# A Fourier mixing layer and a gated feed-forward: DFT-47 of five batches moved into the token steps, and bank claims of two columns

## The chip, the cores and the metric

One core of a Trainium2 chip runs the whole program. The metric is device time in microseconds (us), the median of three runs: 2581.76 us (2578.75 to 2582.05). TensorE (PE) does the matrix products and its weight loads (PEld); VectorE (DVE), ScalarE (ACT) and GpSimd (POOL) work on data between them; SyncE (SP) issues almost all DMAs.

## The reference

Two layers in a row, cut to what matters:

```python
X = np.fft.rfft(x, axis=1)                      # x: 8 batches, 3008 positions, 256 features
Yr = Xr @ w_r - Xi @ w_i + b_r
Yi = Xr @ w_i + Xi @ w_r + b_i
Yr = np.sign(Yr) * np.maximum(np.abs(Yr) - 0.01, 0.0)      # Yi likewise
y = np.fft.irfft(Yr + 1j * Yi, n=3008, axis=1)
h = y.reshape(24064, 256) @ w_in                # w_in: 256 x 2048
out = (h / (1 + np.exp(-1.702 * h))) @ w_out    # w_out: 2048 x 256
```

## The kernel before

The transform of 3008 positions is split into 64 x 47. For one batch it runs in five steps: a DFT of length 47 (step A, `dft47`, L463), whose result goes to a DRAM tensor s1; a DFT of length 64 (step B, products `pa<-kr,br`), which reads s1 back into tiles br; the mixing matrices with the threshold; the inverse DFT of length 64, whose result goes to a DRAM tensor s2; and the inverse DFT of length 47, which is part of `tokens` (L604). `tokens(u)` takes eighth u of all batches' tokens (NU = 8 a batch) from s2 into the transposed tiles th and tl of the feed-forward.

The feed-forward (`Ffn`) goes over 47 blocks of 512 tokens and, in each, over 8 groups of 256 hidden features. `up` makes 12 products of 512 columns into two banks of PSUM (`pa<-th,wi_h` and the like), ScalarE applies the activation, VectorE and ScalarE form sums and split each into a high and a low part (fp32r), and `down` makes 21 products of 256 columns into accumulators po. The last loop (L863) makes 376 such steps. The spectral steps of the next batch stand in a list with a cost each (`spectral`, L478), and the loop takes from it in proportion to the feed-forward steps left, so that the batch is done 16 steps before it is needed. For batches 3 to 7 that list begins with the eight groups of step A at a cost of 1100 each and an empty step of cost 4000. Step A of batches 1 and 2 runs in the start-up (`early`, `do_early`).

Products of small shape run on quarters of the array: `dft47` uses 48 rows by 64 columns in four quarters (four products of 512 columns, in two passes since they are fp32), `tokens` the same with 32 products of 47 columns. Inside `with quarters()` PE's order is the one written. All else is ordered when the program is built: a scheduler places the recorded instructions of each engine by its own timeline, so that products of several stages mix.

The pool `pa` has four banks of PSUM. `bank()` takes one; an instruction that first writes it waits until ScalarE and VectorE have read what was there. So that this wait isn't met inside a quarters group, `claim` (L351) makes a tiny product into the first bank ahead of the group: two columns of output on all 128 rows, with a weight load of 128 columns. `dft47` and `tokens` need two banks each and claim one of them.

Input tiles of step A (xt), of the tokens (ur), and the pairs of the inverse step share three buffers of the tag sx.

Of the kernel before, what the change touches and what calls it, by code (L numbers as in the profile page):

```python
# [25 lines left out]
NU = NJ // 4  # L26
# [90 lines left out]
def fourier_mix_then_gated_ffn(ctx: ExitStack, tc: tile.TileContext, x, w_r, w_i, b_r, b_i, w_in, w_out, pack, kbs, out):  # L117
# [232 lines left out]

    def claim(ps):  # L351

        mm(ps[:, 0:2], wi_h[:, 0, 0:128], wi_h[:, 0, 0:2])

    def dram_views(s1, s2):
        return (s1.rearrange("c (s r) p n j d -> c (r p n j) s d", r=2),
# [106 lines left out]
    def dft47(b, n, t, first=None, other=None):  # L463

        ps = [bank(), bank() if other is None else other]
        with quarters():
            if first:
                first(ps[0])
            for c, p in ((1, 1), (0, 0), (0, 1), (1, 0)):
                mm(ps[p][64 * c:64 * c + 64], kp[64 * p:64 * p + 48], t[c][64 * p:64 * p + 48])  # L470
        s1w = s1s[b].rearrange("c f p n j d -> (c f) p n (j d)")
        for p in range(2):
            ev = buf2("aev").rearrange("p j d -> p (j d)")
            nc.scalar.copy(ev, ps[p])  # L474
            nc.sync.dma_start(s1w[:, p, n], ev)


    def spectral(b, s2):  # L478
        begun = b in s1s
        if not begun:  # L480
            new_s1(b)
        s1r, s2w = dram_views(s1s[b], s2)
        ki, fg, wf_h, wf_l = (parts[n] for n in "ifhl")
        yd = dr.tile([NS, 2, N1, D], F32, name="yd")
        xs, raw, zs, ys = {}, {}, {}, {}

        def pair(name):
            t = buf([128, 2, 512], F32R, name, tag="sx", bufs=3)
            return t[:, 0], t[:, 1]

        def load_x(n):
            if n < 8 and n not in xs:
                xs[n] = xload(b, n, buf([128, 1024], F32, "xt", tag="sx", bufs=3))

        def stage_a(n):
            load_x(n)
            load_x(n + 1)
            dft47(b, n, xs[n], claim)

        def load_b(sp):  # L500

            k = buf([128, 2, 2 * N1], F32, "kr")
            t = buf2("br")
            nc.sync.dma_start(k, kbs[12 + sp])
            for c in range(2):
                nc.sync.dma_start(t[64 * c:64 * c + 64], s1r[c, :, 2 * sp:2 * sp + 2])
            raw[sp] = t, k

        def stage_b(sp):

            if sp == 0:
                load_b(0)
            if sp + 1 < 12:
                load_b(sp + 1)
            co = dft64(*raw.pop(sp))
            zz = buf([128, 2, 6, 128], F32R, "zz")
            split(zz[:, 0], zz[:, 1], co.rearrange("p c v n -> p (c v) n"))
            zs[sp] = zz

        def stage_mix(sp):  # L520

            zz = zs.pop(sp)
            pa, pb = bank(), bank()
            for v, ps in ((2, pa[:, 0:D]), (1, pb[:, 0:D]), (0, pb[:, D:])):
                for c in range(2):
                    mm3(ps, zz[:, 0, 3 * c + v], zz[:, 1, 3 * c + v], wf_h[:, v, c], wf_l[:, v, c], start=c == 0, stop=c == 1)
            v = mixed(pa, pb)
            threshold(v)
            for i in range(2):
                nc.sync.dma_start(yd[2 * sp + i].rearrange("r k e -> k r e"), v[64 * i:64 * i + 64])  # L530

        def load_y(sp):
            ys[sp] = buf2("yr")
            nc.sync.dma_start(ys[sp], yd[2 * sp:2 * sp + 2].rearrange("s r k e -> (r k) s e"))

        def split_y(sp):
            y = ys[sp]
            yh, yl = (t.rearrange("p (s d) -> p s d", s=2) for t in pair("yh"))
            for i in range(2):
                f = fg[:, 2 * sp + i:2 * sp + i + 1]  # L540
                nc.scalar.mul(yh[:, i], y[:, i], f)
                nc.vector.scalar_tensor_tensor(yl[:, i], y[:, i], f, yh[:, i].bitcast(F32), ALU.mult, ALU.subtract)
            ys[sp] = yh, yl

        def stage_inv(sp):
            yh, yl = ys.pop(sp)
            pv = bank().rearrange("p (s d) -> p s d", s=2)
            if sp == 0:
                for i in range(2):
                    mm3(pv[:, i], ki[:, 0, 1 - i], ki[:, 1, 1 - i], yh[:, i], yl[:, i])  # L550
            else:
                mm3(pv, ki[:, 0, 0], ki[:, 1, 0], yh, yl)
            ev = buf2("iev")
            nc.scalar.copy(ev, pv)
            nc.sync.dma_start(s2w[2 * sp:2 * sp + 2].rearrange("s p d -> p s d"), ev)

        steps = []

        def add(cost, step, n, count):
            if 0 <= n < count:  # L560
                steps.append((cost, lambda: step(n)))

        if not begun:
            add(0, load_x, 0, 8)
            for n in range(8):
                add(1100, stage_a, n, 8)
            steps.append((4000, lambda: None))
        for n in range(12 + 5):
            add(900, stage_b, n, 12)
            add(2000, stage_mix, n - 1, 12)  # L570
            add(0, load_y, n - 3, 12)
            add(0, split_y, n - 5, 12)
            add(650, stage_inv, n - 5, 12)
        return steps
# [16 lines left out]
    def first_tokens(u):  # L591
        t = us.pop(u)
        for c in range(2):
# [3 lines left out]
            for k in range(JP * u // TOK, (JP * (u + 1) - 1) // TOK + 1):  # L597
# [3 lines left out]
                n0, n1 = max(0, -a), min(JP, TOK - a)  # L601
                split(*(t2[:, c, a + n0:a + n1] for t2 in ytiles[k]), ps[:, n0:n1])

    def tokens(u):  # L604
        if u < 2:
            return first_tokens(u)
        t = us.pop(u)
        ps = [bank() for p in range(2)]
        pv = [b[:, :JP].rearrange("p (c j n) -> p c j n", c=2, j=4) for b in ps]
        with quarters():  # L610
            claim(ps[0])
            for j in range(4):
                for c in range(4):
                    i = 64 * (c % 2)
                    for p in reversed(range(2)):
                        hs = slice(64 * p, 64 * p + 48)
                        mm(pv[p][i:i + 64, c // 2, j], t[hs, j, 64 * c:64 * c + 64], kz[hs])
        for k in range(JP * u // TOK, (JP * (u + 1) - 1) // TOK + 1):
            if k not in ytiles:
                ytiles[k] = (fbuf([128, 2, TOK], F32R, "th"), fbuf([128, 2, TOK], F32R, "tl"))  # L620
            th, tl = ytiles[k]
            at = [JP * u + 94 * j - TOK * k for j in range(4)]
            js = [j for j in range(4) if 0 <= at[j] and at[j] + 94 <= TOK]
            for p in range(2):
                if js:
                    hi, lo = (t[:, :, at[js[0]]:at[js[0]] + 94 * len(js)].rearrange("p c (j n) -> p c j n", j=len(js))[:, :, :, 47 * p:47 * p + 47]
                              for t in (th, tl))
                    split(hi, lo, pv[p][:, :, js[0]:js[0] + len(js)])
                for j in range(4):
                    a = at[j] + 47 * p  # L630
                    n0, n1 = max(0, -a), min(47, TOK - a)
                    if j not in js and n0 < n1:
                        split(th[:, :, a + n0:a + n1], tl[:, :, a + n0:a + n1], pv[p][:, :, j, n0:n1])
# [133 lines left out]
    def tokens_to(n):  # L767
        nonlocal done
        while done < NB * NU and JP * done < n:
            load_u(done)  # L770
            load_u(done + 1)
            tokens(done)
            done += 1
        load_u(done)

    lx0, one0, a0, lk0, t0, b0, m0, i0 = first_batch(new_s2(0))
    new_s1(1)
# [85 lines left out]
    for n in range(NT * NQ):  # L863
        k, q = divmod(n, NQ)
        if q == 0:
            cur = Ffn(k)
        cur.up(q)
        if n < NQ:
            if n < 7:
                with after("h", "l"):  # L870
                    weights(9 + n)
            do_early(n)
            if n == 6:
                with after("h", "l"):
                    rounded_parts()
        elif not queue and nextb < NB:
            queue = spectral(nextb, new_s2(nextb))
            total, spent, n0 = sum(c for c, _ in queue), 0.0, n
            n1 = NQ * S * nextb // TOK - 16
            nextb += 1  # L880
        while queue and spent < total * (n + 1 - n0) / (n1 - n0):
            c, step = queue.pop(0)
            spent += c
            step()
        need = TOK * (1 + (n + 2) / NQ)
        while queue and need + JP > S * (nextb - 1):
            queue.pop(0)[1]()
        if JP * done < need:
            tokens_to(need)
        if behind is not None:  # L890
            behind[0].down(behind[1])
        behind = (cur, q)
# [36 lines left out]
```

## Time and profile before

| what | value |
|---|---|
| median of three runs | 2581.76 us |
| the profiled execution | 2581.11 us |
| its span, first to last instruction | 2579.3 us |
| granted TensorE clock | 0.996 |
| DMA queues of SyncE, share of the 16 engines | 28.1% |

The span is cut by the page into busy time of engines, the chain that ended last, groups of like instructions and DMA issues. A matmul's duration in it includes its way through the array; how long PE is taken by it is read from the distance between the starts of successive matmuls. The rows that matter are shown in the prediction.

### The profile page before, as it was taken

How to read it: one execution, taken by the hardware profiler on the slowest of the kernel's cores; microseconds unless marked ns; L12 is line 12 of the kernel's file. 1: busy time of each engine (PE TensorE's matmuls, PEld its weight loads, DVE VectorE, ACT ScalarE, POOL GpSimd, SP SyncE). 2: the span in 40 equal slices, each digit the busy share in tenths (PEclk: the TensorE clock that was granted, in tenths of full speed). 3: DMA queues.
4: the chain of work that ended last, by engine and by line, in shares of the span. 5: the costliest groups of instructions: out<-in, count | busy, mean ns of one | idle time of the engine just before them, and what ended most of it. 6: DMA issues, size and time to landing. Idle time of an engine off the chain costs nothing.

```text
span 2579.3 us, 49276 instructions
## 1 busy us (share of the span) xinstructions
PE 2556.0 (99%) x19885; PEld 2267.6 (88%) x19885; DVE 1915.7 (74%) x3240; ACT 1597.1 (62%) x2587; POOL 53.2 (2%) x63
## 2 busy tenths in 40 slices
PE   9899999999999999999999999999999999999999
PEld 7679989999899998999889998899988999889888
DVE  6588877777578775777767776678766787777776
ACT  4566665666666666666666666666666666655555
POOL 0000000000000000000000000000000000000000
PEclk9899999999999999999999999999999999999999
DMA  7653331222513235122341323322243122200000
GB/s 220 198 170 86 100 99 54 71 66 66 164 38 86 83 86 148 54 71 82 110 122 52 91 79 115 103 64 83 73 128 97 56 83 80 60 27 24 15 17 17
DMA packets 163780, 221.81 MB, mean 86 GB/s; under 512 B 18256, under 2 KB 121136, under 8 KB 163552
## 3 DMA queue, kind: packets, MB, share of 16 engines
q1 hardware_dynamic: 161920, 212.83, 28.1%
q0 software_dynamic: 1632, 5.83, 0.7%
q8 instruction: 156, 2.56, 0.4%
q14 instruction: 72, 0.59, 0.1%
HBM read 117.40 MB, written 101.19 MB: 85 GB/s over the span
## 4 chain that ended last, share of the span: by engine, by line
PE 96%; DVE 1%; ACT 1%; DMA 1%; issue 0%; SPq 0%; POOL 0%; POOLq 0%; DVEq 0%; ACTq 0%
PE pa L155 58%; PE po L155 37%; DMA s<-iev 0%; PE pi L155 0%; DMA wf_h<-s 0%; PE wm L155 0%; ACT gb L658 0%; DVE lt L663 0%; PE pt L395 0%; DMA pk<-in_pack 0%; ACT aev L474 0%; DVE lb L150 0%; DVE mv L414 0%; ACT iev L441 0%; DVE aem L283 0%
## 5 line engine op out<-in xcount | busy, mean ns | idle before, releaser
L658 ACT ACTIVATE gb<-pa 128x512 f32<-128x512 f32 x752 | 448.8, 599 | 433.0 <-PE pa L155 430.0
L150 DVE TENSOR_TENSOR lt<-gt,ht 128x1024 fp32r<-128x1024 f32 x367 | 452.1, 1232 | 262.1 <-ACT ht L149 261.0
L155 PE MATMUL pa<-th,wi_h 128*128 128x512 f32 x1504 | 594.1, 395 | 0.2
L155 PE MATMUL pa<-tl,wi_h 128*128 128x512 f32 x1504 | 591.4, 393 | 0.0
L155 PE MATMUL pa<-th,wi_l 128*128 128x512 f32 x1504 | 587.6, 391 | 0.0
L149 ACT CAST ht<-gt 128x1024 fp32r<-128x1024 f32 x367 | 384.4, 1047 | 182.9 <-DVE gt L691 179.7
L689 DVE TENSOR_TENSOR gt<-gb 128x512 f32<-128x512 f32 x367 | 253.2, 690 | 199.4 <-ACT gb L658 191.5
L150 DVE TENSOR_TENSOR lb<-gb,hb 128x768 fp32r<-128x768 f32 x367 | 353.5, 963 | 15.2 <-ACT hb L149 14.7
L155 PEld LDWEIGHTS pa<-th,wi_l 128*128 128x128 f32 x1504 | 283.2, 188 | 57.7
L155 PEld LDWEIGHTS pa<-th,wi_h 128*128 128x128 f32 x1504 | 284.1, 189 | 54.7 <-ACT gb L658 3.2
L149 ACT CAST hb<-gb 128x768 fp32r<-128x768 f32 x367 | 306.4, 835 | 31.3 <-PE po L155 22.2
L155 PEld LDWEIGHTS pa<-tl,wi_h 128*128 128x128 f32 x1504 | 284.4, 189 | 40.5
L155 PE MATMUL po<-lt,wo_0a 128*128 128x256 f32 (+1 forms) x752 | 206.1, 287 | 0.0
L155 PE MATMUL po<-ht,wo_1a 128*128 128x256 f32 (+1 forms) x752 | 204.8, 285 | 0.0
L155 PE MATMUL po<-lt,wo_0b 128*128 128x256 f32 (+1 forms) x752 | 204.0, 287 | 0.0
L155 PE MATMUL po<-ht,wo_1b 128*128 128x256 f32 (+1 forms) x752 | 203.1, 285 | 0.0
L155 PE MATMUL pa<-wf_h,zz 128*128 128x256 f32 x1008 | 202.9, 282 | 0.0
L155 PE MATMUL po<-ht,wo_0a 128*128 128x256 f32 (+1 forms) x752 | 182.3, 288 | 0.0
L155 PE MATMUL po<-ht,wo_0b 128*128 128x256 f32 (+1 forms) x752 | 173.0, 287 | 0.3 <-ACT ht L149 0.3
L155 PEld LDWEIGHTS pa<-wf_h,zz 128*128 128x128 f32 x1008 | 164.9, 189 | 1.4
L690 DVE TENSOR_TENSOR gt<-gb,gt 128x256 f32<-128x256 f32 x367 | 154.6, 421 | 6.9
L155 PE MATMUL po<-hb,wo_0a 128*128 128x256 f32 x552 | 157.6, 293 | 0.0
(170 smaller groups left out, 4663.2 us busy)
## 6 DMA issues: line engine op xcount, KB each, us to landing
s<-aev SPq DMA_DIRECT2D x112, 256.0 KB, 3.5
s<-iev SPq DMA_DIRECT2D x96, 256.0 KB, 2.5
ur<-s SPq DMA_DIRECT2D x124, 192.0 KB, 3.4
out<-o SPq DMA_DIRECT2D x93, 256.0 KB, 2.1
br<-s SPq DMA_DIRECT2D x168, 128.0 KB, 2.9
yd<-mv SPq DMA_DIRECT2D x168, 128.0 KB, 2.4
yr<-yd SPq DMA_DIRECT2D x84, 256.0 KB, 2.9
xt<-in_x SPq DMA_DIRECT2D x80, 192.0 KB, 3.4
```

The source lines that it names most:

```text
L149: nc.scalar.copy(hi, src)
L150: return nc.vector.tensor_tensor(lo, src, hi.bitcast(F32), ALU.subtract)
L155: last[0] = nc.tensor.matmul(ps, lhsT=w, rhs=t, start=start, stop=stop).ins
L658: done_at["g"] = nc.scalar.activation(o, ps.rearrange("p (h n) -> p h n", h=2), AF.Gelu_apprx_sigmoid).ins
L689: nc.vector.tensor_tensor(gt[:, 0:2], b12, gb[:, 0:3:2], ALU.subtract)
L690: nc.vector.tensor_tensor(gt[:, 2], gb[:, 2], gt[:, 0], ALU.subtract)
```

## The change

Three edits. First, `dft47` is taken apart into its products and its output, and `tokens` makes the products of step A for batch b + 2, eighth n, together with the inverse DFT of eighth n of batch b, in one quarters group; a new `load_x` loads their input one token step ahead. Second, `spectral` loses step A and the empty step behind it, and its list for batch 3 and later is made once the tokens of the batch two earlier are done. Third, a claim writes two rows of output instead of 128 (a weight load of two columns), and a merged group claims all four of its banks.

```diff
-        mm(ps[:, 0:2], wi_h[:, 0, 0:128], wi_h[:, 0, 0:2])
+        mm(ps[0:2, 0:2], wi_h[:, 0, 0:2], wi_h[:, 0, 0:2])
...
-            for c, p in ((1, 1), (0, 0), (0, 1), (1, 0)):
-                mm(ps[p][64 * c:64 * c + 64], kp[64 * p:64 * p + 48], t[c][64 * p:64 * p + 48])
+            dft47_products(ps, t)
+        dft47_out(b, n, ps)
+
+    def dft47_products(ps, t):
+        for c, p in ((1, 1), (0, 0), (0, 1), (1, 0)):
+            mm(ps[p][64 * c:64 * c + 64], kp[64 * p:64 * p + 48], t[c][64 * p:64 * p + 48])
+
+    def dft47_out(b, n, ps):
...
-        if not begun:
-            add(0, load_x, 0, 8)
-            for n in range(8):
-                add(1100, stage_a, n, 8)
-            steps.append((4000, lambda: None))
...
+    def load_x(u):
+
+        b, n = u // NU + 2, u % NU
+        if u >= NU and b < NB and u not in steps47:
+            if n == 0:
+                new_s1(b)
+            steps47[u] = b, n, xload(b, n, buf([128, 1024], F32, "xt", tag="sx", bufs=3))
...
+        step = steps47.pop(u, None)
+        if step:
+            b, n, _ = step
+            p47 = [bank() for p in range(2)]
         ps = [bank() for p in range(2)]
...
-            claim(ps[0])
+            for x47 in p47 + ps if step else ps[:1]:
+                claim(x47)
+            if step:
+                dft47_products(p47, step[2])
...
+        if step:
+            dft47_out(b, n, p47)
...
             load_u(done)
-            load_u(done + 1)
+            load_x(done)
+            if done < 2:
+                load_u(done + 1)
             tokens(done)
             done += 1
         load_u(done)
+        load_x(done)
...
-        elif not queue and nextb < NB:
+        elif not queue and nextb < NB and (nextb < 3 or done >= NU * (nextb - 1)):
```

PE, one group of step A of batch 3 before, on its own (`pa<-xt,kp`), and behind it a claim of 128 by 2 between whole products (`po<-..` are down products):

```order
L155 MATMUL pa<-xt,kp 64x512 x4
L155 MATMUL po_7107<-lt,wo_0b 128x256
L155 MATMUL po_7107<-ht,wo_1b 128x256
L155 MATMUL po_7108<-lt,wo_0b 128x256
L155 MATMUL po_7108<-ht,wo_1b 128x256
L155 MATMUL po_7107<-ht,wo_0b 128x256
L155 MATMUL po_7107<-lt,wo_0b 128x256
L155 MATMUL po_7107<-ht,wo_1b 128x256
L155 MATMUL pa<-wi_h 128x2
L155 MATMUL po_7109<-lt,wo_0b 128x256
L155 MATMUL po_7109<-ht,wo_1b 128x256
```

PE, a merged group after (step A of batch 5 with tokens of batch 3; `pa<-kz,ur` are the token products), with the claims ahead of it:

```order
L155 MATMUL pa<-wi_h 2x2 x2
L155 MATMUL po_12287<-hb,wo_0a 128x256
L155 MATMUL po_12287<-lb,wo_0a 128x256
L155 MATMUL po_12287<-hb,wo_1a 128x256
L155 MATMUL po_12287<-hb,wo_0a 128x256
L155 MATMUL po_12287<-lb,wo_0a 128x256
L155 MATMUL po_12287<-hb,wo_1a 128x256
L155 MATMUL pa<-wi_h 2x2
L155 MATMUL po_12287<-hb,wo_0a 128x256
L155 MATMUL pa<-wi_h 2x2
L155 MATMUL pa<-xt,kp 64x512 x4
L155 MATMUL pa<-kz,ur 64x47 x32
```

The products of step A now stand straight ahead of the token products, and four claims stand ahead of the group, at three places. In the built program a claim is an instruction on 128 rows by 32 columns of the array, where it was on 128 by 128; step A and the tokens are on 64 by 64.

SP, the end of step A and the first reads of step B, batch 3 before and batch 4 after (`s1<-aev` writes step A's result, `br<-s1` reads it back for step B):

```order
L475 DMA s1_7427<-aev_7937 128x512
L475 DMA s1_7427<-aev_7940 128x512
L506 DMA br_8201<-s1_7427 64x2x256 x2
L506 DMA br_8206<-s1_7427 64x2x256 x2
L589 DMA ur_8827<-s2_3853 48x1024 x2
```

```order
L455 DMA xt_11385<-in_x 48x1024 x2
L481 DMA s1_7666<-aev_11363 128x512
L481 DMA s1_7666<-aev_11366 128x512
L577 DMA ur_11885<-s2_7720 48x1024 x2
L499 DMA br_11441<-s1_7666 64x2x256 x2
L499 DMA br_11446<-s1_7666 64x2x256 x2
L499 DMA br_11462<-s1_7666 64x2x256 x2
```

The reads follow the last write as before. What moved is PE's side: after, between the last merged group of batch 4 and the first product of step B stand 12 up products and 21 down products, of which the last are these:

```order
L155 MATMUL po_11012<-ht,wo_1b 128x256
L155 MATMUL po_11011<-ht,wo_0b 128x256
L155 MATMUL po_11011<-lt,wo_0b 128x256
L155 MATMUL po_11011<-ht,wo_1b 128x256
L155 MATMUL po_11013<-ht,wo_0b 128x256
L155 MATMUL po_11013<-lt,wo_0b 128x256
L155 MATMUL po_11013<-ht,wo_1b 128x256
L155 MATMUL pa<-kr,br 128x2x64 x8
L155 MATMUL pa<-th,wi_h 128x512
```

Before, several feed-forward steps stood there. Now it is less than two of them.

More of the change, by code (lines that the diff above doesn't have):

```diff
@@ L478, in spectral @@
     def spectral(b, s2):
-        begun = b in s1s
-        if not begun:
-            new_s1(b)
         s1r, s2w = dram_views(s1s[b], s2)
@@ L484, in spectral @@
         yd = dr.tile([NS, 2, N1, D], F32, name="yd")
-        xs, raw, zs, ys = {}, {}, {}, {}
+        raw, zs, ys = {}, {}, {}
         def pair(name):
@@ L489, in pair @@
             return t[:, 0], t[:, 1]
[L491 to L498, printed above, removed]
         def load_b(sp):
@@ L561, in add @@
                 steps.append((cost, lambda: step(n)))
-        if not begun:
-            add(0, load_x, 0, 8)
-            for n in range(8):
-                add(1100, stage_a, n, 8)
-            steps.append((4000, lambda: None))
         for n in range(12 + 5):
@@ L602, in first_tokens @@
                 split(*(t2[:, c, a + n0:a + n1] for t2 in ytiles[k]), ps[:, n0:n1])
+    steps47 = {}
+    def load_x(u):
[4 more added lines that the diff above has]
+            steps47[u] = b, n, xload(b, n, buf([128, 1024], F32, "xt", tag="sx", bufs=3))
     def tokens(u):
```

## The prediction

> **What bounds the kernel now.** I read the page first (busy time by engine, then the chain that ended last), then busy time by stretches, and then the timeline of TensorE around single groups.
>
> ```profile
> span 2579.3 us, 49276 instructions
> PE 2556.0 (99%) x19885; PEld 2267.6 (88%) x19885; DVE 1915.7 (74%) x3240; ACT 1597.1 (62%) x2587; POOL 53.2 (2%) x63
> PE 96%; DVE 1%; ACT 1%; DMA 1%; issue 0%; SPq 0%; POOL 0%; POOLq 0%; DVEq 0%; ACTq 0%
> ```
>
> ```profile
> 700.00:1200.00 500.00, 499.58 (x4010) 450.37 (x4009) 377.34 (x635) 312.62 (x507) 8.38 (x9) 1.00 0.29 83
> ```
>
> The first numbers of the last row are the stretch, its length and PE's busy time: in 500 us PE idles 0.4. VectorE (377 us of 500) and ScalarE (313) have room, and the granted clock is 1.00. So no wait can be removed from the main stretch; what counts is what PE's own instructions cost, switches between tile shapes among it, and any new wait on PE goes to the end undiminished. The profiled execution took 2581.1 us, 0.7 below the median of the runs; the sum goes from 2581.1.
>
> **Prices of a switch.** Start of a group of DFT-47 products in the timeline, PE alone (start, duration, operation, rows*columns of the array, count):
>
> ```profile
> 655.74 0.52 PE L155 MATMUL po<-ht,wo_0b 128*128 128x256 f32 x3
> 656.19 0.66 PE L155 MATMUL pa<-xt,kp 48*64 48x512 f32 x4
> ```
>
> and its end, from a later window:
>
> ```profile
> 656.67 0.61 PE L155 MATMUL pa<-xt,kp 48*64 48x512 f32 x4
> 657.21 0.39 PE L155 MATMUL po<-lt,wo_0b 128*128 128x256 f32 x1
> 657.43 0.28 PE L155 MATMUL po<-ht,wo_1b 128*128 128x256 f32 x1
> 657.55 0.29 PE L155 MATMUL po<-lt,wo_0b 128*128 128x256 f32 x1
> ```
>
> Whole products of 256 columns follow each other at 0.12 us (657.43 to 657.55). The third of the x3 starts at 655.98, the group 0.21 later: **entering costs 0.09**. From the group's second pass (656.67) to the next whole product are 0.54 us, and that one's successor comes after 0.22: the **return costs 0.10** more, since the weight load was not done ahead. What the leaving itself costs shows where DFT-47 products once run straight into token products, without a switch:
>
> ```profile
> 130.05 0.59 PE L155 MATMUL po<-xr,kp 48*64 48x512 f32 x1
> ...
> 130.48 1.10 PE L155 MATMUL pa<-kz,ur 48*64 48x47 f32 x64
> 131.51 0.50 PE L155 MATMUL po<-ht,wo_0a 128*128 128x512 f32 x1
> ```
>
> 0.43 instead of 0.54: **leaving costs 0.11**. I take 0.095 for each change of shape, whichever way, and 0.10 for each return to whole products.
>
> **The claims.** One before, between whole products, and one directly ahead of a group:
>
> ```profile
> 658.03 0.28 PE L155 MATMUL po<-ht,wo_1b 128*128 128x256 f32 x1
> 658.15 0.17 PE L155 MATMUL pa<-wi_h 128*128 128x2 f32 x1
> 658.18 0.36 PE L155 MATMUL po<-lt,wo_0b 128*128 128x256 f32 x1
> 658.38 0.28 PE L155 MATMUL po<-ht,wo_1b 128*128 128x256 f32 x1
> ...
> 695.85 0.39 PE L155 MATMUL pa<-tl,wi_h 128*128 128x512 f32 x1
> 696.08 0.39 PE L155 MATMUL pa<-th,wi_l 128*128 128x512 f32 x1
> 696.30 0.17 PE L155 MATMUL pa<-wi_h 128*128 128x2 f32 x1
> 696.40 0.66 PE L155 MATMUL pa<-xt,kp 48*64 48x512 f32 x4
> ```
>
> The first one costs 0.03 + 0.08 = 0.11 us. The second costs nothing: 0.10 passes to the group, which is the price of the switch anyway. The new claim has two columns, and the built program gives it a shape of its own, 128 rows by 32 columns. The trace before has no such instruction. It has a change in the columns alone, from 64x128 (the inverse of the first batch) to 64x64, beside one to whole products:
>
> ```profile
> 43.47 0.60 PE L155 MATMUL pi<-mv,kt 64*128 64x256 f32 x4
> 43.99 0.48 PE L155 MATMUL pa<-wf,co 128*128 128x256 f32 x1
> ...
> 87.95 0.60 PE L155 MATMUL pi<-mv,kt 64*128 64x256 f32 x4
> 88.47 0.66 PE L155 MATMUL pa<-xp,kp 48*64 48x512 f32 x4
> ```
>
> Both take 0.52 us: a change of columns alone costs as much as a full one. So a new claim between whole products is bounded by 0.03 (its own step at 658.15, no switch) from below and by two changes and a return, 2 x 0.095 + 0.10 = 0.29, from above; less than nothing is excluded, as an instruction stays. I take 0.29 and 0.01 for its short load, since the 64x128 rows are the nearest. The Trainium skill, "TensorEngine Tiling (Array Packing)", Key Properties, says that a change of the tiling mode, unlike one of the tile, drains TensorE. By it the new claim pays 0.29, as in the sum; without it the same 158 stretches of claims would be almost free, which is rival C.
>
> **Sum on PE.** Counted in the built programs: changes of shape 294 before, 451 after (49 fewer entries into quarters, as 40 groups merge and fewer token groups are cut; 156 more into claims from whole products). Returns to whole products 145 before, 193 after. Claims 114 before, 56 of them between whole products; 194 after, in 158 stretches. So: 157 x 0.095 = +14.9; 48 x 0.10 = +4.8; 56 x 0.11 = -6.2; own steps of the new claims 158 x 0.01 + 36 x 0.03 = +2.7. Together **+16.2**. In it the merging alone gives -49 x (2 x 0.095 + 0.10) = -14.2; the claims take it back. The DFT products themselves, their copies and DMAs are the same in number and only stand elsewhere.
>
> **The wait that appears.** Before, the spectral steps of batches 3 to 7 left a step of cost 4000 with no work between the last DFT-47 and the first use of its result. It goes. The chain (ScalarE's copies, the write to DRAM, the read back, the first product of step B) in the timeline of batch 3:
>
> ```profile
> 697.87 1.07 ACT L474 COPY aev<-pa 128x512 f32<-128x512 f32 x2
> ```
>
> ```profile
> 698.48 0.83 SPq L475 DMA_DIRECT2D s<-aev  x2
> 702.45 3.08 SPq L506 DMA_DIRECT2D br<-s  x4
> ```
>
> ```profile
> 719.84 0.27 PE L155 MATMUL pa<-kr,br 128*128 128x128 f32 x1
> ```
>
> ```profile
> DMA to landing us min/median/max: 2.5/2.9/5.3
> ```
>
> From the group's start (696.40) to the first read's issue 6.05 us (batch 7: 1954.21 to 1960.35, 6.14). A tile br needs two reads; the second of the four is issued 0.65 later, the fourth 1.95. With 2.9 to landing the first tile is there at 6.05 + 0.65 + 2.9 = 9.6 and the second at 10.9. Before, the product came at 23.4, so all was hidden.
>
> ```profile
> 1954.21 1.09 PE L155 MATMUL pa<-xt,kp 48*64 48x512 f32 x8
> ```
>
> ```profile
> 1960.35 1.25 SPq L506 DMA_DIRECT2D br<-s  x2
> ```
>
> After, PE's work from the group's start to that product is the DFT products (0.91, that is 0.48 + 0.43), 32 token products (1.03, row 130.48), the return 0.10, 12 up products at 0.23 (2.8; spacing at 695.85) and 16, 21, 23, 25 and 17 down products at 0.12 for batches 3 to 7: 6.8, 7.4, 7.6, 7.8 and 6.9 us. PE therefore waits 2.8, 2.2, 2.0, 1.8 and 2.7, together 11.5. The next tile's products stand right behind (at most four whole products between), wanted at 10.1 to 10.5 and there at 10.9: some 3 more. **+14.5**, with 12.5 at a landing of 2.5 and 26 at 5.3. SP's queue holds this too: ahead of the reads stand two loads xt, the two writes and two loads ur, which fit into the 6 us. Behind the waiting products stand all other PE work, so nothing refills the gap.
>
> **Four banks at once.** The merged group holds all four banks. 18 of the 40 groups are followed at once by an up product that needs the bank of the first copied half.
>
> ```profile
> 660.02 1.09 PE L155 MATMUL pa<-xt,kp 48*64 48x512 f32 x8
> ```
>
> ```profile
> 661.18 1.08 ACT L474 COPY aev<-pa 128x512 f32<-128x512 f32 x2 [1.37 <-PE pa L155]
> ```
>
> ```profile
> L149 ACT CAST ht<-gt 128x1024 fp32r<-128x1024 f32 x367 | 384.4, 1047 | 182.9 <-DVE gt L691 179.7 <-PE pa L155 0.5
> ```
>
> An undelayed copy ends 1.75 us after the group's start (661.18 + 0.59), and the token products run until 1.95: hidden. A cast on ScalarE ahead of it costs up to 1.05. From 0 to 18 x 1.05 = 19; I take a quarter of the cast each, **+4**, as ScalarE is busy 62% but mostly with shorter pieces. The claims' own waits for banks lie behind down products (21 x 0.12 = 2.5 us a step), as before: 0.
>
> **Moved at no cost.** The loads xt are issued a token step ahead (a median of 270 products of PE, before 60), and hold one of the three buffers that they share with ur and the pairs of the inverse step. One is left for 12 pairs in the 310 us of a batch, one in 26 us, so I put this at 0; without that cover 60 inverse products could wait up to a cast, 1.05 us, each, and that belongs to D.
>
> Sum: 16.2 + 14.5 + 4 = +34.7, so 2615.8; I say **2615**.
>
> **Rivals.** B, the switches cost as said but the read is hidden (it lands sooner than the copies suggest): 2581.1 + 16.2 + 4 = 2601. Against it: 6.05 us to the issue alone leave at most 1.8 for issue and landing, and the shortest landing is 2.5.
>
> C, the other side: the claim of 32 columns changes no shape that must drain. For it: the weight load is two columns wide, and the old claim's whole cost was its load. Then the quarters save 14.2, the old claims 6.2, and the new ones cost 194 x 0.01 to 0.03, 2 to 6. With the waits at 11 (14.5 less 5 x 0.3, the copies as early as at 661.18, and 5 x 0.4, landings at 2.5; no bank wait) the time is 2581.1 - 18.4 + 11 = 2574, faster; with all 18.5 of waits 2585. It decides from a claim below 0.05 us, where the 11 and the savings cancel. The section LDWEIGHTS of "TensorE: Matmul & The Clock Gate" in the Trainium skill puts a load at its columns over 1.2 ns, so estimated 1.7 ns for two against 107 for 128; by that alone C would hold, and no row before shows a load of two columns. Against C stand the two equal 0.52.
>
> D, the four banks bind: each of 40 groups makes PE wait half a microsecond more for ScalarE: +20, 2635. For it: 36 claims now stand in pairs or threes, which wait for several banks at one place. Against it: the 0.4 us of idle in 500.
>
> That the change doesn't do what it says: two of the 40 groups stand cut in the program after two token products; that is 2 x 0.29 and in the counts.
>
> **How the numbers follow.** A 0.62, B 0.13, C 0.12, D 0.13. A by itself spans 2603 to 2628 (landing and bank waits at their ends). The range leaves out C and the far part of D: 2594 to 2640. 0.2% is 5.2 us, about what a measurement of this kernel can tell from no change. C splits into faster 0.07 and same 0.05; slower takes A, B and D, 0.88, of which I leave 0.02 to same and 0.01 to faster for what I didn't see.
>
> **What would show it.** Right: whole product to 2x2 claim 0.21 and claim to whole product about 0.10, with 0.22 behind it; some 2 to 3 us of PE idle put down to DMA br before kr,br at five places, some 310 us apart; DFT to token products 0.42. Wrong: claims 0.03 apart from their neighbours (C); no idle before kr,br (B); idle at claims or at up products behind groups put down to ScalarE, over 10 us in sum (D).

## The result, and the profile after

The changed kernel took 2600.49 us (median of 6 runs, 2598.17 to 2601.95), the kernel before in the same runs 2580.64 (2578.75 to 2582.05). The ratio is 1.0074 with a 95% interval of 1.0063 to 1.0086: slower, by 20 us where 34 were forecast.

The page of the changed kernel, its head and its chain:

```profile
span 2596.4 us, 49412 instructions
PE 2551.6 (98%) x19965; PEld 2268.4 (87%) x19965; DVE 1923.4 (74%) x3240; ACT 1595.8 (61%) x2587; POOL 52.2 (2%) x63
...
PE 76%; DVE 2%; DMA 2%; ACT 1%; issue 1%; SPq 0%; POOL 0%; POOLq 0%; DVEq 0%; ACTq 0%
PE pa L155 46%; PE po L155 30%; DMA s<-aev 1%; DMA br<-s 1%; DVE lb L150 0%; DVE gt L696 0%; ACT ht L149 0%; ACT gb L665 0%; ACT aev L480 0%; DVE lt L150 0%; ACT yh L534 0%; DVE tl L150 0%; DVE gt L698 0%; DVE gt L697 0%; DMA xt<-in_x 0%
```

The span grew by 17.1 us while PE was busy 4.4 us less. The chain of before was 96% PE; now write and read of step A's result (`s<-aev`, `br<-s`) stand in it with 1% each. The stretch of the main part says the same, 494.06 us busy of 500 where it was 499.58 (columns as in the prediction):

```profile
700.00:1200.00 500.00, 494.06 (x3999) 443.06 (x3998) 371.05 (x620) 310.67 (x501) 8.89 (x9) 1.00 0.30 88
```

What PE waited for, from the list of waits (us in total, times, the longest):

```profile
PE pa L155 <- DMA br<-s: 14.0, 5, 3.5
...
PE po L155 <- DVE o L763: 3.0, 6, 1.1
...
PE po L155 <- ACT o L756: 2.4, 2, 1.2
...
PE po L155 <- DVE o L762: 1.6, 2, 1.1
...
PE po L155 <- DVE o L759: 0.8, 1, 0.8
PE pa L155 <- ACT aev L480: 0.7, 1, 0.7
```

and from the same list of the kernel before, the two lines that answer the first and the last:

```profile
PE pa L155 <- DMA br<-s: 0.7, 1, 0.7
PE pa L155 <- ACT aev L474: 0.7, 1, 0.7
```

Five waits for the read-back of step A are the largest item, and of a kind that was forecast. The lines `po <- o` were not: a down product there waits until the last block's accumulators are copied out. The line `aev`, where a wait for the four banks would show, has its one wait of before. Claims and a merged group, in the timeline of PE (the claim's tile of 128 x 32 is printed 128*2):

```profile
1063.65 0.28 PE L155 MATMUL po<-hb,wo_1a 128*128 128x256 f32 x1
1063.77 0.17 PE L155 MATMUL pa<-wi_h 128*2 128x2 f32 x1
1063.80 0.36 PE L155 MATMUL po<-hb,wo_0a 128*128 128x256 f32 x1
1064.23 0.17 PE L155 MATMUL pa<-wi_h 128*2 128x2 f32 x1
1064.33 1.09 PE L155 MATMUL pa<-xt,kp 48*64 48x512 f32 x8
1065.24 1.10 PE L155 MATMUL pa<-kz,ur 48*64 48x47 f32 x64
1067.43 0.39 PE L155 MATMUL po<-hb,wo_0a 128*128 128x256 f32 x1 [1.10 <-DVE o L763]
```

The claim comes 0.12 us after the whole product and passes to the next one in 0.03; nothing drains. And it costs what the 128-column claim cost: the product behind it still shows 0.36 us. Directly ahead of the group it is again free (0.10 to the group), though this one comes some 0.2 us late: 0.43 behind a product that the next usually follows after 0.20. The merged group ends in a wait of 1.10 us for VectorE, of the unforeseen kind.

An account of PE makes this whole. The distances between successive starts of matmuls, from 175 us on, were sorted by what stands there: entries, exits and small products of quarters; claims; what exceeds the usual distance by over 0.15 us (waits); the rest. The account is of the two profiled executions, 2598.17 and 2581.11 us, whose spans are 17.1 us apart; the medians are 19.9 apart.

| us | before | after | difference | forecast |
|---|---|---|---|---|
| quarters, with entry and return | 135.5 | 116.7 | -18.8 | -14.2 |
| claims | 6.6 | 12.6 | +6.0 | +30.4 |
| waits at `kr,br` | 1.1 | 15.0 | +13.9 | +14.5 |
| other waits | 2.6 | 15.3 | +12.7 | +4 |
| the rest, with the start | 2423.7 | 2427.1 | +3.4 | 0 |

The claims' forecast is the +16.2 of the switches less the merge's -14.2. The rest holds a surprise, told last: a lower clock behind some waits.

### The profile page after: what moved, and what is told of

Same layout as the page of the kernel before. It is cut to its first block, busy times and chain, and to the rows that moved or that the text cites. A ratio compares the mean times of both kernels' runs of the same rounds, so it can differ in the third digit from the quotient of the medians.

```text
span 2596.4 us, 49412 instructions
## 1 busy us (share of the span) xinstructions
PE 2551.6 (98%) x19965; PEld 2268.4 (87%) x19965; DVE 1923.4 (74%) x3240; ACT 1595.8 (61%) x2587; POOL 52.2 (2%) x63
## 4 chain that ended last, share of the span: by engine, by line
PE 76%; DVE 2%; DMA 2%; ACT 1%; issue 1%; SPq 0%; POOL 0%; POOLq 0%; DVEq 0%; ACTq 0%
PE pa L155 46%; PE po L155 30%; DMA s<-aev 1%; DMA br<-s 1%; DVE lb L150 0%; DVE gt L696 0%; ACT ht L149 0%; ACT gb L665 0%; ACT aev L480 0%; DVE lt L150 0%; ACT yh L534 0%; DVE tl L150 0%; DVE gt L698 0%; DVE gt L697 0%; DMA xt<-in_x 0%
```

## The experiments

Each was timed in five rounds against the kernel before; the figure is the median, then the ratio with its interval. Waits are sums from the same account.

**The short claim alone**, in the kernel before:

```diff
-        mm(ps[:, 0:2], wi_h[:, 0, 0:128], wi_h[:, 0, 0:2])
+        mm(ps[0:2, 0:2], wi_h[:, 0, 0:2], wi_h[:, 0, 0:2])
```

> The kernel before with the claims of two columns alone (nothing merged, no step moved). Theory 1 (from the trace after, where a claim between whole products takes 0.12 to its start, 0.03 to the next product and 0.20 behind it, as before): a claim costs 0.11 us in either form, so the time stays within 0.1% of before and a lone claim keeps the 0.03 and 0.20. Theory 2 (of the prediction, a drain at each change to 128 rows by 32 columns): about 56 x 0.18 + 57 x 0.1, some 15 us more, +0.6%. Theory 3 (the short load saves the claim): 56 x 0.08 = 4.5 us less.

2579.11 us, 0.9991 [0.9983, 1.0]. Its claims take 6.5 us in the account, the old ones 6.6. Timeline of PE:

```profile
656.11 0.28 PE L155 MATMUL po<-ht,wo_1b 128*128 128x256 f32 x1
656.23 0.17 PE L155 MATMUL pa<-wi_h 128*2 128x2 f32 x1
656.25 0.36 PE L155 MATMUL po<-lt,wo_0b 128*128 128x256 f32 x1
656.45 0.28 PE L155 MATMUL po<-ht,wo_1b 128*128 128x256 f32 x1
```

0.12 + 0.02 + 0.20 from product to product, where two whole products need 0.24 without a claim: 0.10 us. A weight load of 2 columns instead of 128 gains nothing, and a tile of 128 x 32 costs no change of shape. Why the shorter load gains nothing shows in the weight loads, here first those of this run and then those around the old claim in the kernel before:

```profile
656.11 0.09 PEld L155 LDWEIGHTS pa<-wi_h 128*2 128x2 f32 x1
656.23 0.19 PEld L155 LDWEIGHTS po<-lt,wo_0b 128*128 128x128 f32 x1
...
658.03 0.19 PEld L155 LDWEIGHTS pa<-wi_h 128*128 128x128 f32 x1
658.15 0.19 PEld L155 LDWEIGHTS po<-lt,wo_0b 128*128 128x128 f32 x1
```

The claim's own load did fall, from 0.19 to 0.09 us, but it lies beside the product ahead of the claim. The load of the product behind begins in both forms only when the claim does (656.23 and 658.15) and lasts 0.19, while the claim's own step is 0.03 long: that load is what is left uncovered. Both prices that the prediction weighed for the claim, 0.29 and about 0.02, are wrong.

**The empty step put back**, in the changed kernel, at the head of the spectral steps of batches 3 to 7:

```diff
+        if b > 2:
+            steps.append((4000, lambda: None))
```

> The changed kernel with the empty step of cost 4000 put back at the head of the spectral list of batches 3 to 7. Theory 1: PE's five waits for the read of step A's result (14.0 us in the trace after, and 1.4 us of half clock behind the longest) go, the rest stays: 15 us less, 2585 us. Rival: the wait only moves (to the block ends or the end of a batch, since the list is denser): no change within 3 us.

2586.07 us, 1.002 [1.0011, 1.0028]: 14.4 us are back. The group of the first products of step B by shape, of the changed kernel:

```profile
L155 PE MATMUL pa<-kr,br 128*128 128x128 f32 x672 | 95.7, 284 | 16.8 <-DMA br<-s 14.0 <-issue 2.7
```

and with the empty step:

```profile
L155 PE MATMUL pa<-kr,br 128*128 128x128 f32 x672 | 93.5, 279 | 3.5 <-issue 3.3 <-DMA br<-s 0.2
```

The wait for the read is gone, and most of the loss with it. What remains are other waits: 20.0 us, more than the 15.3 without the empty step.

**The empty step taken out of the kernel before**, the other half of the same test:

```diff
-            steps.append((4000, lambda: None))
```

> The kernel before with its empty step of cost 4000 taken out, and nothing else. In the built program the first product of step B then follows the last group of step A after some 9.6 us of PE's work (8.6 for batch 7); in the trace after, the read was there 9.9 to 11.1 us after the group's start. Theory 1 (that chain is what PE waits for): five waits of 0.3 to 1.8 us at kr,br, 3 to 8 us in all, 2584 to 2589. Rival (the wait of the changed kernel comes of its merged groups or its queue of loads): no waits at kr,br, 2580 to 2582.

2590.13 us, 1.0036 [1.0023, 1.0048]: 9.6 us over the kernel before in these runs. From its list of waits:

```profile
PE pa L155 <- DMA br<-s: 5.8, 5, 2.6
```

One of these five, of 0.7 us, stands in the kernel before as well. The new ones are at batches 3, 6 and 7, one at each of the first two and two at the last; batches 4 and 5, where waits were expected too, have none. By the account the new waits are 6.0 us of the 11.5 by which this profiled execution's span is longer than before's, and half the clock behind the longest (told last) is 1.7 more. So the same deletion makes PE wait for the read in the old order too.

**Two claims a group**, one for each half, in the changed kernel:

```diff
-            for x47 in p47 + ps if step else ps[:1]:
+            for x47 in p47[:1] + ps[:1] if step else ps[:1]:
```

> The changed kernel with two claims a merged group (the first bank of each pair) instead of four. Theory 1: 80 claims at 0.11 us are paid on PE, so 6 to 9 us less. Rival: what the claims took up comes back as waits inside the group, at 0.2 to 0.6 us each for some of 40 groups: no change within 3 us, with idle before xt or kz products in the trace.

2593.82 us, 1.0049 [1.0036, 1.0061]. By shape:

```profile
L155 PE MATMUL pa<-wi_h 128*2 128x2 f32 x114 | 17.7, 177 | 1.2 <-ACT gb L665 1.2
```

80 claims fewer save 3.9 us (12.6 to 8.7), but the quarters take 11.4 us more (116.7 to 128.1): without a claim on every bank whole products move into the merged groups again (in the trace 10 runs of small products hold both DFT and token products, where the changed kernel has 40), and each piece pays its entry and return. The waits at `kr,br` fell to 8.0 us with the products that moved. The claims are what keeps a merged group in one piece.

**Both at once**, two claims and the empty step:

> Both, the empty step and two claims a group. If the two costs are apart, the savings add: 21 to 24 us less than the changed kernel, 2577 to 2580 us, just below before. If the merge's own gain of some 19 us on PE is real, the time can go below before only as far as the new waits at the accumulators (8 us in the trace after) let it.

2587.08 us, 1.0025 [1.0015, 1.0034]: no better than the empty step alone. The expectation fell: the two gains don't add. The first was mostly a shorter read wait, which the second takes away anyway; quarters 128.4, claims 8.1, waits 15.1.

**The other waits: the place of the token groups?** With the empty step, the need for tokens was set so that the last groups of a block aren't all due at its end:

```diff
-        need = TOK * (1 + (n + 2) / NQ)
+        need = TOK * (k + 1 + (min(8, q + 2) / NQ if q > 1 else 0))
```

> The changed kernel with the empty step, and with token groups held off the ends of a block of 512 tokens (none is started in the first two and the last feed-forward step of a block; in the built program none stands between the last down product of a block and the first of the next, where 9 stood with the empty step alone). Theory 1 (a merged group there puts ScalarE's and VectorE's reads of the accumulators behind its own copies, and PE's first down products wait for them: 8 to 9 us in the trace after): the waits for o and the combine fall to 1 or 2, and with 16 more changes into quarters (3 to 4 us more) the time is 2580 to 2583. Rival (the waits come from fuller ScalarE and VectorE everywhere): they stay, 2588 to 2592.

2587.17 us, 1.0025 [1.0014, 1.0036]. Waits, those at `kr,br` included, 18.4 us instead of 20.5: those of the first down products (`hb`, `ht`) halved, from 9.3 to 4.5, and others rose, at up products from 3.3 to 4.7. The place of the groups explains a part at most, and the time did not fall. (The profiled execution was the slowest of its seven, 2591.7 us.)

**The merge undone**, with the empty step; the DFT products are again a group of their own ahead of the token's:

```diff
-            b, n, _ = step
-            p47 = [bank() for p in range(2)]
+            b, n, t47 = step
+            dft47(b, n, t47, claim)
...
-            for x47 in p47 + ps if step else ps[:1]:
-                claim(x47)
-            if step:
-                dft47_products(p47, step[2])
+            claim(ps[0])
```

> The changed kernel with the empty step and the merge alone undone: step A stays in the token steps but in its own quarters group with one claim, ahead of the token group with one claim. Theory 1 (the merge saves 17 to 20 us of switches on PE and costs 6 of claims and some 9 of waits at the accumulators since it holds four banks): switches come back, claims and waits go, about 2586 + 19 - 6 - 9 = 2590. Rival (the switches saved are worth nothing, the merge only costs): below 2580.

2585.91 us, 1.0021 [1.0012, 1.003], the same as merged. Merged, quarters take 14.9 us less (115.7 against 130.6), claims 4.3 more, waits 8.6 more: the saving is real, and it is eaten (the rest of the account, 3.0 more, takes the last 2; 1.7 of it is half the clock behind a wait of 1.98 us, which the unmerged kernel has at the same product, 1.97 us long, without that loss).

**A long empty step**, 12800, merged and unmerged.

```diff
-            steps.append((4000, lambda: None))
+            steps.append((12800, lambda: None))
```

> The changed kernel with an empty step of cost 12800 (the eight groups at 1100 and the 4000 that stood there before), so that the other spectral steps of batches 3 to 7 fall where they fell before. Theory 1 (the waits for the accumulators come of the spectral steps' new places against the ends of the blocks): the waits at po fall from 13 us (with 4000) to under 5, 2577 to 2580. Rival (they come of the copies of step A in the token steps, or of the four banks): they stay, 2584 to 2588.

> As the last, with the merge undone (step A in the token steps in a group of its own, one claim each). If merging is worth its switches less claims once the waits are as before, this is 6 to 10 us above the last one. If the four banks make the waits, it is below it. It differs from the kernel before only in where step A's groups stand and in the short claims: 2580 to 2584 if that place costs nothing.

2607.96 us, 1.0103 [1.0089, 1.0117], and 2605.14, 1.009 [1.0076, 1.0103]. Neither the theory's time nor the rival's came. The list of waits of the merged one:

```profile
PE pa L155 <- ACT gb L667: 8.1, 4, 3.0
...
PE pa L155 <- ACT yh L534: 3.7, 3, 1.5
PE po L155 <- DVE lb L150: 3.3, 3, 1.8
...
PE po L155 <- ACT o L758: 2.5, 2, 1.3
PE po L155 <- DVE o L765: 2.4, 3, 1.7
...
PE po L155 <- DVE o L761: 1.6, 1, 1.6
```

The waits grew to 35.7 and 23.7 us, now also at ScalarE's activations (`gb`). More distance between step A and the next spectral steps did not remove the waits. The two longest at `gb`, 2.7 and 3.0 us, are not those of a busy ScalarE. SyncE, ScalarE and PE at the first of them:

```profile
1420.55 0.85 SPq L481 DMA_DIRECT2D s<-aev  x2
1421.45 0.43 SPq L527 DMA_DIRECT2D yr<-yd  x1
...
1426.13 0.91 ACT L534 ACTIVATE yh<-yr,fg__1648 128x256 fp32r<-128x256 f32 x2 [5.31 <-DMA yr<-yd]
...
1427.57 0.79 PE L155 MATMUL pa<-th,wi_h 128*128 128x512 f32 x1 [2.68 <-ACT gb L667]
```

SyncE issues a load of the inverse step (`yr`) straight behind the two writes of step A's result. ScalarE stands idle 5.3 us for it, the activation `gb` behind it comes late, and PE waits; the second is alike. Whether the load would have come sooner without these writes was not tried.

The unmerged run differs from the kernel before in where step A's groups and their loads stand, and in the short claims, which alone cost nothing. The other spectral steps are as dense as there: from the first `kr,br` product of batch 4 to the last are 189 us, before 196, in the changed kernel 238. Yet the kernel before has 2.6 us of other waits, and this one is 24.6 us slower than it. So density alone does not make the waits. What differs is step A's work among the other steps, which stand some 20 us later than before.

A longer empty step leaves fewer feed-forward steps for the same spectral work: its own cost is 42600 a batch, so 4000 squeezes it into 91% of the steps and 12800 into 77%.

**A short empty step**, 1500 (97%), merged and unmerged:

> The changed kernel with an empty step of cost 1500 put back after step A, where the kernel before had 4000. Theory (the waits at TensorE's accumulators grow with the density of the spectral steps, so a longer empty step costs more of them, while 1500 is just long enough for the read of step A's result to land): waits of TensorE for the read 0 to 1 us in all, its other waits 15 to 17 us (the changed kernel had 15, the one with 4000 had 20), 2581 to 2584 us. Rival (those waits come with step A standing close to the other steps and not with the pause's length): the same 20 us of other waits and 2586 us as with 4000. If 1500 is too short, the read shows again, at 5 us or more.

> The same empty step of cost 1500, with the DFT products of batches 3 to 7 a list of their own ahead of the token's group, as before. Theory: waits for the read 0 to 1 us, other waits 9 to 11 us (12 with 4000), 2582 to 2584 us, so that the merge is worth a microsecond at most either way. Rival: 2586 us as with 4000. If the merge's saved switches come through once the pause is short, this run is 5 us or more slower than the merged one beside it.

Merged 2578.96 us, 0.999 [0.9981, 0.9999]; unmerged 2581.12, 1.0001 [0.9992, 1.001]. Both came out a little below what was expected. The list of waits of the merged one:

```profile
PE pa L155 <- DMA wf_h<-s: 5.4, 1, 5.4
PE po L155 <- DVE o L765: 4.6, 6, 1.9
...
PE pa L155 <- ACT aev L480: 1.4, 2, 0.8
...
PE po L155 <- ACT o L758: 1.2, 1, 1.2
PE po L155 <- DVE o L761: 1.1, 2, 0.8
...
PE pa L155 <- DMA br<-s: 0.4, 1, 0.4
```

The read is hidden (0.4 us) and the other waits are fewer than with 4000 (the first line is of the start-up and stands in every run). By the length of the empty step, waits other than at `kr,br`:

| empty step | merged, us and waits | unmerged, us and waits |
|---|---|---|
| 0 | 2600.49, 15.3 | not run |
| 1500 | 2578.96, 14.7 | 2581.12, 8.1 |
| 4000 | 2586.07, 20.0 | 2585.91, 11.3 |
| 12800 | 2607.96, 35.7 | 2605.14, 23.7 |

At 1500 the merge is worth 2 us, though the two intervals overlap; at 4000 nothing; at 12800 it costs 3, with overlapping intervals again. So the change with an empty step of 1500 is 0.1% faster than the kernel before, the fastest version found, beside the short claim alone (0.9991), whose account differs from before's by nothing but 1.2 us of waits. Neither is a gain of 0.2%.

## Why the prediction was right, and where not

**The direction and the range held** because the largest real cost, the read-back, was found in the profile of before, and the range in part by luck. With the claims at the 6.0 that they cost, the other terms of the prediction give 2581.1 - 14.2 + 6.0 + 14.5 + 4 = 2591: slower, but below its range of 2594 to 2640. Waits and a clock that it did not have made up the difference. The sum did not hold: 34.7 against 17.2 in the account. Two of its figures do not follow from their own terms, without bearing on this: a quarter of a cast at 18 groups is 4.7 and not 4, and with both ends of landing and bank waits A spans 2610 to 2642 and not 2603 to 2628.

**The claims, +30.4 against +6.0.** This is the step that failed: "I take 0.29 and 0.01 for its short load, since the 64x128 rows are the nearest." Those rows change columns between tiles of 128 and 64, and do cost; the step to a tile of 32 columns on all rows costs nothing, in the changed kernel and in the short claim alone. A Key Property in "TensorEngine Tiling (Array Packing)" of the Trainium skill, that a change of the tiling mode drains TensorE, was weighed there; for 128 x 128 to 128 x 32 the trace does not agree (0.12 us in, 0.03 out, as for the claim in one mode). Rival C fell as well: it took the old claim's cost for its load, and a claim with a load a sixty-fourth as wide costs the same 0.10 to 0.11 us; what is paid is the load of the product behind. What the claims did cost is their number, 80 more.

**The merge, -14.2 against -18.8.** The mechanism was right: from the DFT's second pass straight into token products takes 0.43 us (1064.81 to 1065.24), as in the row that priced it. It was sized too small by 4.6, for which no cause was looked for, and the run with two claims a group shows what it hangs on: the claims hold the groups together.

**The read-back wait, +14.5 against +13.9.** Shown from both sides, by putting the empty step back (14.4 us) and by taking it out of the kernel before (9.6 us, of which some 6 are waits for the read). The five waits come where the prediction had them, but its parts erred both ways. The first tile's waits were 3.3, 3.7, 2.2, 2.1 and 3.5 us, together 14.8 for the 11.5 forecast, since the read was there 9.8 to 11.1 us after the group's start instead of 9.6; the second tile, put at 3, waited almost nothing.

**Four banks, +4 against 0, and +12.7 elsewhere.** The place was wrong: in the changed kernel no wait was added at the up products behind a merged group. (With the empty step back it does show, as `pa <- aev`: 2.5 us in four waits with 4000, 0.8 with 1500.) Instead PE waits at down products, some 11 us, most of it for the accumulators to be copied out, and a little at the inverse step. Eight of the thirteen waits over 0.3 us there stand within 10 us behind the start of a merged group, of which one comes every 40 us; with 4000 and the merge undone none of six stands so near to a group of step A. And undoing the merge removes 7 to 12 us of waits, so the four banks have a part in it; step A's work beside the other spectral steps has the rest, as the unmerged runs wait too (8.1 us with 1500, 2.6 before). That they grow with the length of the empty step from 1500 on is shown for two forms of the kernel and three lengths each; that the denser spectral steps do it together with step A is argued. For the two longest waits at 12800 the late load `yr` is shown. Which instruction is late at the others, and why at these places, stays open.

**Moved loads, 0:** no wait of PE for `xt` shows. Whether the buffer that they hold delays the inverse step was not tried.

## What to carry to other kernels

An empty step in a schedule can be the cover of a DMA's way there and back: before it is deleted, work out from the trace what then lies between write and first use, and try a shorter one, since here 0 cost 15 us of waiting, 1500 almost none, and 4000 another 7 us of time. The price of a switch between tile shapes should be measured for the very pair of shapes: the nearest pair gave 0.29 us and the length of the load 0.02, where 0.11 was measured. On an engine that is busy 99% a saving in its own instructions shows only as far as the other engines and the loads keep up with the new order.

## What the runs showed of the hardware that was not expected

Behind some waits PE came back at half its clock. Busy time of the changed kernel by stretches of 3.41 us, the sixth figure from PE's on being the granted clock:

```profile
675.07:678.48 3.41, 0.42 (x4) 0.45 (x5) 0.99 (x2) 0.00 (x0) 0.00 (x0) 1.00 0.54 167
678.48:681.89 3.41, 3.41 (x19) 3.41 (x18) 0.43 (x1) 1.96 (x3) 0.00 (x0) 0.50 0.36 113
...
1630.80:1634.21 3.41, 1.46 (x13) 1.28 (x13) 2.07 (x3) 1.04 (x1) 0.00 (x0) 1.00 0.67 197
1634.21:1637.62 3.41, 3.41 (x19) 3.41 (x18) 0.85 (x2) 1.92 (x4) 0.00 (x0) 0.50 0.37 101
...
1948.24:1951.65 3.41, 1.85 (x15) 1.62 (x13) 2.32 (x4) 1.43 (x2) 0.00 (x0) 1.00 0.24 87
1951.65:1955.06 3.41, 1.67 (x14) 1.70 (x15) 0.00 (x0) 0.50 (x2) 0.00 (x0) 1.00 0.71 213
1955.06:1958.48 3.42, 3.42 (x26) 3.20 (x25) 2.78 (x4) 2.26 (x4) 0.00 (x0) 1.00 0.87 211
```

After the wait of 3.3 us the clock was 0.50 for 3.41 us, a loss of 1.7 us, and so it was after the one of 2.1 us; after 3.5 us at 1950 it stayed at 1.00. Of the five read waits, those of 3.3, 3.7 and 2.1 us lost 1.7 us each, those of 2.2 and 3.5 none: 5.1 us together. That is more than the growth in the last row of the account (+3.4); the remainder of that row, the start among it, is 1.7 less. So a wait costs more than its length, and whether it does is not set by its length alone. Where it falls matters: the three stretches at half the clock begin at 678.48, 999.33 and 1634.21 us, 94 and 186 times 3.413 us apart, as on a fixed grid. In the stretch of that grid ahead of each, PE was busy for 0.42, 1.60 and 1.46 us. The waits of 2.2 and 3.5 us fell across a border of the grid, and PE was busy for at least 1.67 us on either side. In the other runs the limit is not sharp: with 12800, merged, a stretch with 1.76 us of work was followed by the half clock and one with 1.59 was not. Products of 512 columns behind the wait of 3.7 us show it one by one:

```profile
1001.12 0.63 PE L155 MATMUL pa<-th,wi_l 128*128 128x512 f32 x1
1001.55 0.63 PE L155 MATMUL pa<-th,wi_h 128*128 128x512 f32 x1
...
1004.79 0.39 PE L155 MATMUL pa<-tl,wi_h 128*128 128x512 f32 x1
1005.03 0.39 PE L155 MATMUL pa<-th,wi_l 128*128 128x512 f32 x1
```

They start 0.43 us apart, those from 1004.79 on 0.24. The same loss of 1.7 us followed one wait of 2.6 us where the empty step was taken out of the kernel before, and one of 1.9 us with the empty step of 1500. "TensorE: Matmul & The Clock Gate" of the Trainium skill, Part 1, tells of a clock halved after an idle window of some 3.4 us, in windows that run freely, until the engine was busy for another. A loss of 1.7 us is half the clock for 3.4 us, so the traces agree on the length and on half, and the common grid of the starts is what windows that run freely would give; that waits of 1.9 and 2.1 us set it off is less idling than the page asks for.
